# Retention of seven batch entries in 64x64 array tiles, with half of the heads shifted by 64 tokens

## The chip, the cores and the metric

The kernel runs on one core of a Trainium2 chip. A core has five engines with instruction queues of their own: TensorE (matmuls into PSUM), VectorE, ScalarE and GpSimd (element-wise work), and SyncE (here only DMA issue). They meet through semaphores. The metric is the device time of one execution in microseconds (us); lower is better. The kernel before takes 315.73 us (median of 3 runs, 315.45 to 316.26).

## The reference

Two layers follow one another. The first is a retention, an attention without a softmax, over 8 batch entries, 8 heads, 576 tokens and a head width of 64:

```
scores = q @ k^T / sqrt(64)
D[i, j] = gamma_h ** (i - j)  if i >= j  else 0,   gamma_h = 1 - 2 ** (-5 - h)
x       = (scores * D) @ v            # per batch entry and head
```

The heads of a token are then laid side by side, which gives x as 4608 tokens by 512. The second layer is an MLP:

```
h = x @ w_in          # 512 -> 2048
g = h * sigmoid(1.702 * h)
out = g @ w_out       # 2048 -> 512
```

All inputs and the output are float32; the kernel computes its matmuls in bf16.

## The kernel before, in words

**Retention.** A batch entry b is worked in five chunks c of 128 tokens (the last has 64), which makes 40 steps n = 5b + c. The decay gamma^(i-j) is split: v is scaled by gamma^(-j)/8 (`scale_v`, L249 to L255), and the result for token i is scaled by gamma^i when it leaves PSUM (`evac_o`, L348 to L355). Within a chunk, `scores` (L273) multiplies keys by queries, `mask_s` (L286) zeroes what lies above the diagonal, and `values` (L294) multiplies by the scaled v. What earlier chunks contribute comes through a 64x64 state per head, k^T v, which `values` accumulates in PSUM over the chunks of an entry ("state", L316); ScalarE copies it to SBUF (`evac_z`, L344), and the next chunk multiplies it by its queries ("inter", L327). Each state pair of two heads lies block-diagonally in a 128x128 tile `zs`, so that inter is four full matmuls. k and q must be transposed first: in steps 0 to 13 by TensorE (`transposes`, L257, then `evac_t` by ScalarE, L270), from step 14 on by DMAs that SyncE issues (`dma_turn`, L357).

**Tile shapes on TensorE.** Scores use 64 rows by 128 columns of the array, two matmuls side by side (L282); masked scores times v and state use 128 rows by 64 columns, again in pairs (L303, L316); inter, transposes and the MLP use the full array.

**MLP.** It runs over nine blocks of 512 tokens. `hidden` (L400) computes 128 of the 2048 hidden features for a block, four matmuls, and ScalarE applies the activation. `project` (L438) makes a quarter of the sum for 128 output rows, four matmuls; after the fourth quarter VectorE copies the result to SBUF and SyncE stores it.

**Order.** Every engine's queue is written out by hand, by the order of the calls; the helper `Rec` derives the waits from what each operation reads and writes, and drops a wait between two operations of TensorE. `burst(n)` (L383) puts a retention step between MLP units: scores and mask of step n, values of step n-1, the transposes of a later step, the evacuation of step n-1, and `scale_v(n+1)`. Steps 0 to 3 run first; then hidden of block 0, with no burst; then the projection of block 0, with steps 4 to 7 between its 16 units (the table `between`, L541); then hidden of block 1 in halves, with bursts 8 to 13 (L548); then `region(c)` for blocks 2 to 8, which interleaves the projection of block c-1 with hidden of block c and spreads the bursts that the next block needs evenly over 32 units. The projection of block 8 ends the kernel.

**Loads.** GpSimd issues all loads (`load`, L177, one DMA of 128 tokens and 8 heads for each of q, k, v; `load_w_in`, L187, four DMAs; `load_w_out`). Slots for three batch entries exist (`NST`); entry b+3 is loaded when entry b is finished. Between w_in(1) and w_in(2) GpSimd itself scales v of steps 1 to 3.

## Time and profile before

| | |
|---|---|
| median of 3 runs | 315.73 us (315.45 to 316.26) |
| profiled execution | 314.2 us, its span 312.3 us, granted clock 0.999 |
| TensorE busy | 304.2 us, 97% of the span |
| VectorE, ScalarE, GpSimd busy | 119.6, 131.7, 110.5 us |
| hidden (L407, L425) on the chain that ended last | 34.2% + 1.4% and 3.1% + 1.4% of the span |
| projection (L441) on it | 34.3% + 4.1% + 1% |
| retention matmuls on it (L282, L303, L316, L327, L264) | 3.5%, 3.7%, 1%, 2.8%, 1.6% |
| DMA engines | busy over 90% in the first 22 of 40 slices, 20 to 30% or less after |

A row of a timeline gives the start in us from the span's start, the length in us, the engine, the line of the kernel, the operation, the tiles (out<-in), the shape and the count of instructions that are merged in it; for a matmul 64*128 are the rows and columns of the array that it uses, and the last shape is what streams through. Square brackets hold idle time before the row and what ended it. In the list of waits the three numbers are the total in us, how often, and the longest. Matmuls overlap: a single one of 512 columns lasts 379 ns from start to end, but the next starts 216 ns after it, so the times of a stage are read from starts.

### The profile page before, as it was taken

How to read it: one execution, taken by the hardware profiler on the slowest of the kernel's cores; microseconds unless marked ns; L12 is line 12 of the kernel's file. 1: busy time of each engine (PE TensorE's matmuls, PEld its weight loads, DVE VectorE, ACT ScalarE, POOL GpSimd, SP SyncE). 2: the span in 40 equal slices, each digit the busy share in tenths (PEclk: the TensorE clock that was granted, in tenths of full speed). 3: DMA queues.
4: the chain of work that ended last, by engine and by line, in shares of the span. 5: the costliest groups of instructions: out<-in, count | busy, mean ns of one | idle time of the engine just before them, and what ended most of it. 6: DMA issues, size and time to landing. Idle time of an engine off the chain costs nothing.

```text
span 312.3 us, 5547 instructions
## 1 busy us (share of the span) xinstructions
PE 304.2 (97%) x2379; PEld 154.9 (50%) x2379; DVE 119.6 (38%) x177; ACT 131.7 (42%) x241; POOL 110.5 (35%) x138
## 2 busy tenths in 40 slices
PE   7889999999999999999999999999999999999995
PEld 3444456887544444444444444444444444444442
DVE  5650068655354333333354333333353331110011
ACT  8676235776434443444433333434444443333300
POOL 9999798788566765333400000000000000000000
PEclk9999999999999999999999999999999999999999
DMA  9999999999999999999992223213230010001011
GB/s 72 150 201 202 183 151 203 174 151 149 130 167 173 173 162 175 166 161 129 174 118 42 74 64 83 60 53 83 69 92 36 34 37 34 34 36 66 35 69 67
DMA packets 148697, 34.59 MB, mean 111 GB/s; under 512 B 139968, under 2 KB 144064, under 8 KB 148672
## 3 DMA queue, kind: packets, MB, share of 16 engines
q0 software_dynamic: 116736, 18.36, 88.2%
q1 hardware_dynamic: 31936, 15.87, 23.4%
q8 instruction: 19, 0.31, 0.4%
q14 instruction: 6, 0.05, 0.0%
HBM read 36.70 MB, written 9.44 MB: 148 GB/s over the span
## 4 chain that ended last, share of the span: by engine, by line
PE 92%; POOL 3%; DMA 2%; issue 0%; ACT 0%; DVE 0%; POOLq 0%
PE psU L441 34%; PE psH L407 34%; PE psH L441 4%; PE psO L303 4%; PE psS L282 4%; PE psH L425 3%; PE psO L327 3%; DMA w_in_sb<-in_moe_w_in_dram 2%; PE psT L264 2%; PE psU L425 1%; PE psU L407 1%; POOL st_q L184 1%; POOL st_k L184 1%; PE psZ L316 1%; PE psO L441 1%; POOL st_v L184 1%
## 5 line engine op out<-in xcount | busy, mean ns | idle before, releaser
L412 ACT ACTIVATE gT<-psH 128x512 bf16<-128x512 f32 x123 | 73.6, 598 | 129.2 <-PE psH L407 129.2
L407 PE MATMUL psH<-xT,w_in_sb 128*128 128x512 bf16 x492 | 120.9, 379 | 1.1 <-DMA w_in_sb<-in_moe_w_in_dram 1.1
L441 PE MATMUL psU<-w_out_sb,gT 128*128 128x512 bf16 x496 | 121.9, 379 | 0.0
L291 DVE TENSOR_TENSOR sm<-psS,mask 128x1024 bf16<-128x1024 f32 (+1 forms) x40 | 44.7, 1116 | 100.1 <-PE psS L282 100.1
L407 PEld LDWEIGHTS psH<-xT,w_in_sb 128*128 128x128 bf16 x492 | 47.5, 98 | 57.0 <-DVE xT L353 1.1
L441 PEld LDWEIGHTS psU<-w_out_sb,gT 128*128 128x128 bf16 x496 | 47.4, 98 | 53.6 <-ACT gT L412 0.3
L184 POOL DMA_DIRECT2D st_k<-in_k_dram x40 | 34.8, 870 | 27.0 <-PE psO L327 17.6
L449 DVE COPY osb<-psU 128x512 f32<-128x512 f32 x31 | 21.4, 691 | 55.6 <-PE psU L441 54.7
L184 POOL DMA_DIRECT2D st_q<-in_q_dram x40 | 35.0, 875 | 10.6 <-issue 10.2
L184 POOL DMA_DIRECT2D st_v<-in_v_dram x40 | 34.8, 874 | 8.1 <-issue 4.7
L254 DVE TENSOR_TENSOR st_v<-st_v,vfac 128x512 bf16<-128x512 bf16 x37 | 25.2, 681 | 18.3 <-DMA st_v<-in_v_dram 18.3
L344 ACT ACTIVATE zs<-psZ 64x256 bf16<-64x256 f32 x64 | 24.2, 378 | 12.4 <-PE psZ L316 11.4
L353 DVE TENSOR_TENSOR xT<-psO,gq 128x512 bf16<-128x512 f32 (+1 forms) x38 | 23.8, 627 | 5.6 <-PE psO L327 4.9
L270 ACT ACTIVATE qk<-psT 128x1024 bf16<-128x1024 bf16 x14 | 14.4, 1025 | 17.5 <-PE psT L264 17.5
L282 PEld LDWEIGHTS psS<-qk 64*128 64x128 bf16 x320 | 8.7, 94 | 17.2 <-issue 12.3
L282 PE MATMUL psS<-qk 64*128 64x128 bf16 (+1 forms) x320 | 15.0, 213 | 1.6 <-ACT qk L270 1.6
L303 PE MATMUL psO<-sm,st_v 128*64 128x128 bf16 (+1 forms) x304 | 14.9, 220 | 0.0
L441 PE MATMUL psH<-w_out_sb,gT 128*128 128x512 bf16 x64 | 14.8, 379 | 0.0
L425 PE MATMUL psH<-xT,w_in_sb 128*128 128x256 bf16 x88 | 11.4, 273 | 0.0
L303 PEld LDWEIGHTS psO<-sm,st_v 128*64 128x64 bf16 x304 | 9.2, 109 | 4.3 <-issue 0.6
L327 PE MATMUL psO<-qk,zs 128*128 128x128 bf16 (+1 forms) x120 | 11.0, 215 | 0.0
L441 PEld LDWEIGHTS psH<-w_out_sb,gT 128*128 128x128 bf16 x64 | 6.1, 98 | 7.2 <-ACT gT L412 0.3
(57 smaller groups left out, 127.6 us busy)
## 6 DMA issues: line engine op xcount, KB each, us to landing
out_dram<-osb SPq DMA_DIRECT2D x36, 256.0 KB, 2.2
st_q<-in_q_dram POOLq DMA_DIRECT2D x32, 128.0 KB, 17.3
st_k<-in_k_dram POOLq DMA_DIRECT2D x32, 128.0 KB, 17.3
st_v<-in_v_dram POOLq DMA_DIRECT2D x32, 128.0 KB, 17.3
w_in_sb<-in_moe_w_in_dram POOLq DMA_DIRECT2D x4, 512.0 KB, 8.4
w_out_sb<-in_moe_w_out_dram POOLq DMA_DIRECT2D x4, 512.0 KB, 13.8
st_q<-in_q_dram POOLq DMA_DIRECT2D x8, 64.0 KB, 18.7
st_k<-in_k_dram POOLq DMA_DIRECT2D x8, 64.0 KB, 18.6
```

What stands on the lines that cost most here:

```text
L184: R.op("POOL", lambda e, d=d, s=s: e.dma_start(d, s), w=[(nm, sl, c)], dma=(nm, sl, c))
L254: R.op(eng, lambda e: e.tensor_tensor(t, t, f, ALU.mult), r=["vfac"], w=[("v", sl, c)])
L282: i = e.matmul(psS[:, hh, hp, 0:N], t[rows, 1, hp, :], t[rows, 0, hp, 0:N])
L291: R.op("DVE", lambda e: e.tensor_tensor(o, i, m, ALU.mult), r=["mask"], w=[("sm", n % 3)], ps=["S"])
L303: i = e.matmul(po[64 * hh : 64 * hh + 64, hp, 0:N], st_v[:, sl, c, 64 * h : 64 * h + 64], sm[n % 3][:, hh, hp, 0:N], start=(hp == 0), stop ...
L344: R.op("ACT", lambda e, rows=rows: e.activation(zs[c % 2][rows, :, rows], psZ[rows, :, 0:64], AF.Copy), w=[("zs", c % 2, hh)], ps=["Z"])
L353: R.op("DVE", lambda e: e.tensor_tensor(xT[:, :, t0 : t0 + N], po[:, :, 0:N], gq[:, c, :, 0:N], ALU.mult), r=[("gq", min(c, 1))], w=[("xT" ...
L407: i = e.matmul(bank.ap(), w_in_sb[:, a, 128 * f : 128 * f + 128], xT[:, a, 512 * c : 512 * c + 512], start=(a == 0), stop=(a == 3))
L412: R.op("ACT", lambda e: e.activation(gT[c % 2][:, f, :], bank.ap(), AF.Gelu_apprx_sigmoid), w=[("gT", c % 2, f)], ps=[key])
L425: m = e.matmul(bank[:, 256 * i : 256 * i + 256], w_in_sb[:, a, 128 * (f + i) : 128 * (f + i) + 128], xT[:, a, a0 : a0 + 256], start=(a == ...
L441: i = e.matmul(bank, gT[c % 2][:, f, 128 * r : 128 * r + 128], w_out_sb[:, f, :], start=(f == 0), stop=(f == NF - 1))
L449: R.op("DVE", lambda e: e.tensor_copy(osb[m].ap(), bank), w=[("osb", m)], ps=[key])
```

## The change

Batch entry 0 keeps its form, but for the order of heads and for inter, which becomes eight matmuls of 128x64 instead of four full ones. For entries 1 to 7:

- k and v of heads 4 to 7 are loaded 64 tokens late, each load in two DMAs of four heads: rows 64 to 127 of a chunk's slot hold the first 64 tokens of the chunk for these heads, rows 0 to 63 of the next slot its second 64. So the first half of the keys of heads 0 to 3 lies in the upper 64 partitions while that of heads 4 to 7 lies in the lower ones, and matmuls of both groups use different quarters of the array at the same time.
- `scores` works in 64x64 tiles: first 64 keys by 128 queries, then the second 64 keys by the last 64 queries; the quarter of the square above the diagonal is left out. It needs the transposed k of step n+1 too. `mask_s` uses two masks.
- `values_quarters` puts masked scores times v, state and inter of a step in two parts (first and second 64 keys), all in 64x64 tiles. The scores of the next step stand between them, and the second part waits for the first by a semaphore of TensorE itself (`own`). It needs v and k of chunk c+1 too.
- The state of one chunk alone is made in PSUM; VectorE adds it up over the chunks in `zacc` (float32) and copies it to `zq` (bf16). ScalarE no longer takes part.
- The order: 15 steps are transposed by TensorE instead of 14; transposes and DMA transposes are asked with one step more to go; steps 4 to 9 stand at other units. `burst(n)` holds `values_quarters(n-1)`, with `scores(n)` in its middle.
- w_in is loaded in four DMAs for each former one (its rows are reordered with the heads), and w_in(1) moves behind GpSimd's scaling of v. Each `load` of k or v of entries 1 to 7 is two DMAs, not one.
- VectorE makes a second mask, a second set of scale factors, and zeroes of two tiles at the start.

The core of the diff:

```diff
-PE_TURNS = 14
+PE_TURNS = 15
+        if own:
+            deps.append(own)
-            elif d.eng == eng and eng in ("PE", "SP"):
+            elif d.eng == eng and eng in ("PE", "SP") and d is not own:
...
+        def load_shifted(b, c, nm, src, dst):
+            sl = b % NST
+            parts = []
+            for u, (lo, hi) in enumerate(((0, ROWS[c]), (64 if c == 0 else 0, 128))):
+                d = dst[lo:hi, sl, c, 256 * u : 256 * u + 256].rearrange("p (h d) -> p h d", d=DH)
+                t0 = 128 * c - 64 * u
+                s = src[b, 4 * u : 4 * u + 4, t0 + lo : t0 + hi, :].rearrange("h p d -> p h d")
+                parts.append((d, s))
+            R.op("POOL", lambda e: [e.dma_start(d, s) for d, s in parts],
+                 w=[(nm, sl, c)], dma=(nm, sl, c), parts=2)
...
         def load_w_in(i):
-            s = moe_w_in.rearrange("(a p) n -> p a n", p=128)[:, :, 512 * i : 512 * i + 512]
-            R.op("POOL", lambda e: e.dma_start(w_in_sb[:, :, 512 * i : 512 * i + 512], s),
-                 w=[("w_in", i)], dma=("w_in", i))
+            parts = []
+            for u in range(2):
+                for t in range(2):
+                    d = w_in_sb[64 * t : 64 * t + 64, 2 * u : 2 * u + 2, 512 * i : 512 * i + 512]
+                    r0 = (4 * u + 2 * t) * DH
+                    s = moe_w_in[r0 : r0 + 2 * DH, 512 * i : 512 * i + 512]
+                    parts.append((d, s.rearrange("(j p) n -> p j n", j=2)))
+            R.op("POOL", lambda e: [e.dma_start(d, s) for d, s in parts],
+                 w=[("w_in", i)], dma=("w_in", i), parts=4)
...
+            def quarters_fn(e):
+                for last in range(1 if c == 4 else 2):
+                    for t in range(2):
+                        for u in range(2):
+                            keys = later if u and last else now
+                            kb = half(u ^ last)
+                            for j in range(2):
+                                i = e.matmul(psS[kb, j, 2 * t + u, 64 * last : N],
+                                             keys[half(j), 1, 2 * u + t, kb],
+                                             now[half(j), 0, 2 * u + t, 64 * last : N])
+                return i
...
+            def part(last):
+                def fn(e):
+                    if c < 4 or last == 0:
+                        for j in range(2):
+                            for u in range(2):
+                                rows, cc = half(u ^ last), c + (u & last)
+                                for t in range(2):
+                                    h = 4 * u + 2 * t + j
+                                    i = e.matmul(psV[half(t), u, 128 * j + 64 * last : 128 * j + N],
+                                                 st_v[rows, sl, cc, 64 * h : 64 * h + 64],
+                                                 s[rows, j, 2 * t + u, 64 * last : N],
+                                                 start=(last == 0 and j == 0), stop=False,
+                                                 skip_group_check=True)
+                    if c < 4:
+                        ...
+                                    i = e.matmul(psV[half(j), u, 256 + 64 * t : 320 + 64 * t],
+                                                 st_k[rows, sl, cc, hs], st_v[rows, sl, cc, hs],
+                                                 start=False, stop=False, skip_group_check=True)
+                    if c > 0:
+                        for u in range(2):
+                            j = u ^ last
+                            for t in range(2):
+                                i = e.matmul(psV[half(t), u, 128 * j : 128 * j + N],
+                                             zq[(c - 1) % 2][half(j), 2 * u + t, :],
+                                             qk[n % NQK][half(j), 0, 2 * u + t, 0:N],
+                                             start=False, stop=(last == 1), skip_group_check=True)
+                    return i
+                return fn
+            ...
+            first = R.op("PE", part(0), r=r, ps=["O", "Z"])
+            if n + 1 < NSTEP:
+                intra(n + 1)
+            R.op("PE", part(1), r=r, ps=["O", "Z"], own=first)
...
+            if n >= NC:
+                ...
+                if c == 0:
+                    R.op("DVE", lambda e: e.tensor_copy(acc, new), w=["zacc"], ps=["O", "Z"])
+                elif c < 3:
+                    R.op("DVE", lambda e: e.tensor_tensor(acc, acc, new, ALU.add),
+                         w=["zacc"], ps=["O", "Z"])
+                if c < 3:
+                    R.op("DVE", lambda e: e.tensor_copy(z, acc), r=["zacc"], w=[("zq", c % 2)])
+                else:
+                    R.op("DVE", lambda e: e.tensor_tensor(z, acc, new, ALU.add),
+                         r=["zacc"], w=[("zq", c % 2)], ps=["O", "Z"])
+                return
...
         def burst(n):
-            if n < NSTEP:
+            if n > NC:
+                values_quarters(n - 1)
+            else:
                 intra(n)
-            values(n - 1)
-            if n + 1 < PE_TURNS:
-                transposes(n + 1)
-                evac_t(n + 1)
+                values(n - 1)
+            if n + 2 < PE_TURNS:
+                turn(n + 2)
...
         load_w_in(0)
-        load_w_in(1)
         for n in range(1, 4):
             scale_v(n, "POOL")
-        load_w_in(2)
-        load_w_in(3)
+        for i in range(1, 4):
+            load_w_in(i)
...
-        between = {6: lambda: turn(4), 8: burst_4, 10: lambda: burst(5), 11: lambda: burst(6),
-                   13: burst_7}
+        between = {5: turn_4, 6: burst_4, 8: lambda: turn(6), 10: lambda: burst(5),
+                   11: lambda: burst(6), 13: burst_7}
```

In the new order `turn_4` is turn and scaling of step 4, `burst_4` the scores of step 4 with turn and scaling of step 5, and `burst_7` the values of step 6 with the scores of step 7, the evacuation, the turn of step 9 and the scaling of step 8.

## The prediction

> **What bounds the kernel now.** I read the page first, then TensorE's waits, then its timeline at one retention step of the steady part, then VectorE's timeline where steps are packed, then the loads.
>
> Page: engines, and the chain that ended last.
> ```profile
> span 312.3 us, 5547 instructions
> PE 304.2 (97%) x2379; PEld 154.9 (50%) x2379; DVE 119.6 (38%) x177; ACT 131.7 (42%) x241; POOL 110.5 (35%) x138
> ...
> PE 92%; POOL 3%; DMA 2%; issue 0%; ACT 0%; DVE 0%; POOLq 0%
> ```
> What TensorE waited for in the whole span:
> ```profile
> PE psS L282 <- ACT qk L270: 1.6, 4, 0.6
> PE psH L476 <- DVE idle L206: 1.2, 1, 1.2
> PE psH L407 <- DMA w_in_sb<-in_moe_w_in_dram: 1.1, 1, 1.1
> ```
> TensorE is the bound: it waits under 5 us, all before 47 us. Time saved in its queue is time saved, unless a wait takes its place. One steady step, TensorE's timeline (start, length, line, tiles, count):
> ```profile
> 206.50 0.59 PE L407 MATMUL psH<-xT,w_in_sb 128*128 128x512 bf16 x2
> 207.02 0.40 PE L282 MATMUL psS<-qk 64*128 64x128 bf16 x8
> 207.35 0.41 PE L303 MATMUL psO<-sm,st_v 128*64 128x128 bf16 x8
> 207.60 0.29 PE L316 MATMUL psZ<-st_v,st_k 128*64 128x64 bf16 x8
> 207.82 0.40 PE L327 MATMUL psO<-qk,zs 128*128 128x128 bf16 x4
> 208.06 0.38 PE L441 MATMUL psU<-w_out_sb,gT 128*128 128x512 bf16 x1
> ```
> The second L407 starts at 206.50+0.59-0.38 = 206.71; such a matmul occupies 0.216 us (eight in 1.73 us), so the array is free at 206.93, and the next MLP matmul starts at 208.06: the step costs 1.13 us. Subtracting a matmul's own 0.216, 0.219 and 0.196 us gives the last starts of each group. Four pairs of 128 columns (L303) go by at 0.06 us a pair, pairs of 64 columns (L316) at 0.031 (three intervals in 0.094). Between groups of unlike tile shape lies 0.09 us (206.93 to 207.02; L282 to L303; L316 to L327): three switches, 0.28 us of the 1.13. Read alike, the five steps of a batch cost now: 0.80 (burst n with n%5=0), 0.89 (1), 1.13 (2), 1.13 (3), 1.02 (4).
>
> VectorE between 54 and 57 us:
> ```profile
> 54.43 1.22 DVE L291 TENSOR_TENSOR sm<-psS,mask 128x1024 bf16<-128x1024 f32 x1 [0.52 <-PE psS L282]
> 55.57 0.68 DVE L353 TENSOR_TENSOR xT<-psO,gq 128x512 bf16<-128x512 f32 x1
> 56.17 0.68 DVE L254 TENSOR_TENSOR st_v<-st_v,vfac 128x512 bf16<-128x512 bf16 x1
> ```
> 2.4 us a step. There a step comes every 3.3 to 4.2 us, in the steady part every 6 to 8. GpSimd's timeline, and the list of DMA issues from 23 to 35 us (count, size, median us to landing):
> ```profile
> 11.96 1.60 POOL L189 DMA_DIRECT2D w_in_sb<-in_moe_w_in_dram  x2
> 13.98 3.08 POOL L254 TENSOR_TENSOR st_v<-st_v,vfac 128x512 bf16<-128x512 bf16 x3 [0.42 <-DMA st_v<-in_v_dram]
> ```
> ```profile
> st_k<-in_k_dram POOLq DMA_DIRECT2D x4, 128.0 KB, 16.4
> ```
> Loads land 16 us after issue though issued 0.87 apart: the DMA engines set the landing, not GpSimd. k of entry 1 lands at 40.7, 43.4, 46.0, 48.9 and 51.6 (issue plus 16.4 to 17).
>
> **The change, steady part (bursts 14 to 40).** Price of a group of four 64x64 tiles: no row has the shape. From below, all four run together, as both pairs of rows (L282) and pairs of columns (L303) do: 0.06 us per 128 columns, 0.031 per 64. From above, two at a time: 0.12 and 0.062. I take the lower: the two pairings use different sides of the array, and a pair's starts lie 4 ns apart, so four need 14 of the 31 ns. Then a burst with values of chunk 1 or 2:
> - switch in 0.09;
> - first part 0.24: two 128-column groups of masked scores times v, two 64-column state groups, one 128-column group of inter;
> - scores 0.18: two groups of 128 and two of 64 columns, where the masked half is gone;
> - wait of the second part on the first: its last matmul ends 0.16 after its slot, a waiting engine starts 0.04 to 0.06 later (8.17 to 8.23 after L270), the scores cover 0.18: 0.05 with the refill. Behind it stand the second part and all MLP work;
> - second part 0.18 (four 64-column groups, one of 128); switch out 0.09.
>
> Sum 0.84 against 1.13: -0.28, twice per batch. Chunk 0 (no inter): 0.72 against 0.89, -0.17. Chunk 3 with the 64-row scores, which cover less of the wait (0.15 bare): 0.84 against 1.02, -0.18. Chunk 4: 0.54 against 0.80, -0.25. Per batch -1.16; bursts 15 to 39 -5.8; burst 14 -0.2, burst 40 (nothing in its wait) +0.1: **-5.9**.
>
> A rule of the Trainium skill speaks against this: "TensorE: Matmul & The Clock Gate", section "Wait — 56ns, not 53.3ns?", lets no two matmuls start less than about 25 ns apart. By it the 56 matmuls of such a burst would take 1.4 us, and the kernel would end near 332 us. L316 starts eight in 0.094 us, 13 ns apart, so the floor does not hold across tiles.
>
> ScalarE loses L344 (24.2 us), which nothing waits for in the steady part. VectorE gains two operations for chunks 0 to 2, one for chunk 3: 128x256, 0.42 us each by L353's 128x256 form at most, 0.27 by the memset of that size at least; I take 0.42+0.35. At a step every 6 to 8 us the idle VectorE hides it. The transposing DMAs are asked one step earlier; at 200 to 250 us they land 2.5 us after issue: hidden.
>
> **The change, before 82 us.** Batch 0's inter goes from four full matmuls to four column pairs, same time, and lies before the w_in landing. New constants on VectorE (8 small operations and 2 memsets, about 2 us) fit the 2.8 us that it idles before 8.7.
>
> w_in: each of four loads becomes four, and three now stand behind GpSimd's scaling (13.98 to 17.06). An issue takes 0.87 for 1024 rows and 0.68 for 512; by that slope 0.5 for 128, by no slope 0.8. With 0.5, GpSimd is at w_in(1) at 17.4 and done with it at 19.5, landing near 22.3; it is needed at 23.0. First MLP matmul +0.2 (0 to 0.8). The twelve extra DMAs and the split k and v loads each cost the engines 0 to 0.15 us: I shift the loads by 0.8 (0.2 to 2).
>
> Bursts 6 to 13 save by the same table -1.9; the turn of step 14 joins TensorE, 0.45: **-1.5**.
>
> New waits, 38 to 77 us. scale_v(n+1), last of VectorE's step, was used two bursts later; now the next burst's first part needs it, since chunk n+1's lower half enters. So mask, evacuation, two state operations and scaling (2.4+0.75 = 3.2 us from the scores) must fit between neighbouring scores and first part. Between bursts 5 and 6 lies one unit (0.86) and a turn; also two output copies: 0.8 wait. Bursts 6 to 7, two units: 0.7. Bursts 8 to 9, two half units of 0.87: 0.65. Elsewhere three: 0 to 0.1. Turns are also asked earlier: turn(4) 0.86 earlier meets its landing, 0.5; scores(4) one unit, not two, after their turn, while ScalarE needs 1.03: 0.35; turn(6), reached at 43.6, against 43.4+0.8: 0.6; turn(8) 0.2. Together **+3.9** (1.5 to 6.5).
>
> Burst 14 needs step 15's k, whose DMA is issued after burst 12 (72.7) instead of a burst later than needed; a turn's two DMAs are issued 1.25 us apart, and those issued between 66 and 100 us land 7.2 to 9.2 after issue (median 7.6): k at 81.2 to 83.2, needed at 81.2: **+1.0** (0 to 2).
>
> Sum: 0.2-1.5+3.9+1.0-5.9 = **-2.3**. The profiled execution took 314.2 (span 312.3); the median of the runs is 315.7, 1.5 above it. 314.2-2.3 is 311.9, as a median **313.4**.
>
> **Rivals.**
> - Two at a time: a burst of chunk 1 or 2 has six 128-column and eight 64-column groups, +0.6 less the wait that this hides, so about +0.27 against before; per batch +1.1 instead of -1.16, +11 over the steady part, +2.5 early: **327**. For: no 64x64 tile in the trace. Against: both kinds of pair overlap.
> - Weights: 64-column groups as slow as 128-column ones, because a 64-column weight load takes 110 ns (L303) and four are wanted per 31 ns. +0.03 for some seven groups a burst: +5.5 steady, +0.9 early: **319.8**. It decides against the change from 10 ns a group on (2.3 us over some 240 groups). Against: L316's loads already overlap in pairs.
> - Loads: an issue costs 0.8 whatever its size. w_in ends 3 us later in the queue, hidden(0) starts 0.6 late and waits 0.6 for w_in(1), k of chunks 3 and 4 lands 1.7 late, 2.7 more in all: **316.1**, no change.
> - The waits before 82 us turn out hidden (state operations at 0.27, no DMA shift): 1.5 instead of 4.9: **310.0**.
>
> **How the numbers follow.** Forecast 0.52 (own range 311 to 316), two at a time 0.10, weights 0.14, loads 0.14, waits hidden 0.10. Under 0.3% (1 us) a measurement can't tell from no change. Faster: 0.40 of the forecast, 0.10, 0.01 of the weights: 0.51. Same: 0.07 and 0.06: 0.13. Slower: 0.36. Range 310 to 320, which leaves out the first rival and some of the second.
>
> **What would show it.** Per steady burst the MLP gap 0.84 instead of 1.13; 64*64 matmuls starting 4 ns apart in fours; a second part starting 0.21 us after the first's last slot; TensorE waits on scale_v in bursts 6, 7 and 9, on st_k before 50 us and on qk near 82. Wrong if a 64-column group takes over 0.04, or if waits on VectorE persist in the steady part.

## The result, and the profile after

The kernel after takes 319.62 us (median of 4 runs, 318.45 to 320.56) against 315.59 us for the kernel before beside it on the same chip: a ratio of 1.0132, with a 95% interval of 1.0083 to 1.0182. The forecast was faster, 313.4 us; it came out slower. The profiled execution took 318.45 us with a span of 316.6, so the span grew by 4.3 us where the prediction's sum said -2.3.

The kernel's lines have moved: scores are L331 (old form) and L342 (64x64), values L381, L393 and L400, the mask L362, scale_v L301, the transposes L311, hidden L554, project L588, the output copy L596, the state's sum and its bf16 copy L472 to L479, w_in's load L220.

From the page of the kernel after: span, engines, and the chain that ended last.

```profile
span 316.6 us, 7233 instructions
PE 301.2 (95%) x3187; PEld 150.4 (47%) x3187; DVE 137.4 (43%) x235; ACT 112.2 (35%) x186; POOL 159.7 (50%) x220
...
PE 81%; POOL 9%; DMA 5%; DVE 3%; issue 0%; POOLq 0%
```

TensorE is busy 3.0 us less than before, and yet the span is longer: the chain now goes 9% through GpSimd (3% before), 5% through a DMA and 3% through VectorE. What TensorE waited for, in the kernel after (total us, times, longest):

```profile
PE psT L311 <- DMA st_k<-in_k_dram: 2.7, 2, 2.5
PE psV L381 <- DVE st_v L301: 2.3, 3, 0.9
PE psH L554 <- DMA w_in_sb<-in_moe_w_in_dram: 1.9, 2, 1.5
PE psS L331 <- ACT qk L317: 1.6, 4, 0.6
PE psU L554 <- DMA w_in_sb<-in_moe_w_in_dram: 1.5, 1, 1.5
```

Before, the list had 1.6 us on ScalarE, 1.2 at the start and 1.1 on w_in. New are waits on k, above all of entry 0's last chunk (2.7), and on scale_v (2.3); w_in costs 2.3 us more. All of this lies before 67 us; behind it nothing is listed at all.

One retention step of the steady part in the kernel after, the same step (n%5 = 2) as the prediction read at 206.5 us; TensorE's timeline, with start, length, line, tiles and count:

```profile
211.01 1.03 PE L554 MATMUL psH<-xT,w_in_sb 128*128 128x512 bf16 x4
211.96 0.31 PE L381 MATMUL psV<-sm,st_v 64*64 64x128 bf16 x8
212.10 0.23 PE L393 MATMUL psV<-st_v,st_k 64*64 64x64 bf16 x8
212.16 0.23 PE L400 MATMUL psV<-qk,zq 64*64 64x128 bf16 x4
212.22 0.34 PE L342 MATMUL psS<-qk 64*64 64x128 bf16 x16
212.46 0.26 PE L381 MATMUL psV<-sm,st_v 64*64 64x64 bf16 x8
212.55 0.23 PE L393 MATMUL psV<-st_v,st_k 64*64 64x64 bf16 x8
212.61 0.23 PE L400 MATMUL psV<-qk,zq 64*64 64x128 bf16 x4
212.77 0.60 PE L588 MATMUL psU<-w_out_sb,gT 128*128 128x512 bf16 x2
```

The last L554 starts at 211.01+1.03-0.38 = 211.66 and frees the array 0.216 later, at 211.87. The next MLP matmul starts at 212.77: the step costs 0.90 us, where it cost 1.13. Two groups of four 128-column tiles (L381 at 211.96 to L393 at 212.10) and two of four 64-column tiles (L393 to L400) take 0.14 and 0.06 us. Four tiles do run together.

So the steady part is faster, and the time was lost earlier. Where it went, read from the starts of the same work in the two traces (burst 14 is the first burst of the steady part; the MLP matmul ahead of it ends at 78.78 us before and 86.04 after):

| stretch | change of the span |
|---|---|
| to the start of the projection of block 0 (33.39 us before, 36.22 after) | +2.8 |
| turn(4) and turn(5) waiting for k | +2.7 |
| three waits on scale_v, 53 to 66 us | +2.3 |
| all else from there to burst 14 | -0.5 |
| burst 14 to the end (233.5 us before, 230.6 after) | -3.0 |
| sum | +4.3 |

The first two rows are the loads. Busy time by stretches of 4 us in the kernel before and in the kernel after; the last three columns are TensorE's granted clock, the DMA engines' busy share and the GB/s that they moved:

```profile
16.00:20.00 4.00, 2.62 (x45) 1.62 (x43) 3.37 (x6) 3.51 (x8) 4.00 (x6) 1.00 1.23 204
20.00:24.00 4.00, 4.00 (x20) 1.84 (x19) 0.67 (x2) 2.51 (x5) 4.00 (x7) 1.00 1.23 199
24.00:28.00 4.00, 4.00 (x21) 1.77 (x19) 0.00 (x0) 2.85 (x5) 4.00 (x6) 1.00 1.23 202
28.00:32.00 4.00, 4.00 (x20) 1.86 (x19) 0.00 (x0) 2.67 (x6) 4.00 (x5) 1.00 1.24 205
```

```profile
16.00:20.00 4.00, 2.14 (x65) 1.56 (x58) 3.27 (x5) 3.36 (x7) 4.00 (x7) 1.00 0.68 100
20.00:24.00 4.00, 3.63 (x16) 1.49 (x16) 0.97 (x2) 2.32 (x6) 4.00 (x8) 1.00 1.08 149
24.00:28.00 4.00, 3.63 (x16) 1.49 (x16) 0.00 (x0) 2.41 (x5) 4.00 (x7) 1.00 1.07 111
28.00:32.00 4.00, 2.70 (x13) 1.29 (x14) 0.00 (x0) 1.64 (x3) 4.00 (x7) 1.00 1.18 188
```

Before, the engines moved some 203 GB/s without a break. After, they fall short by 104, 50, 91 and 17 GB/s in these four stretches. Times 4 us that is 1,050 KB, or 5.2 us of a queue that moves 203 GB/s. Everything behind it in the queue comes later by that much: k of entry 0's chunk 4 lands at 43.93 us instead of 38.46 (the last completion of that load in the trace), which is 5.5 us, and turn(4) waits for it.

GpSimd's timeline in the kernel after shows what feeds that queue:

```profile
11.96 2.49 POOL L220 DMA_DIRECT2D w_in_sb<-in_moe_w_in_dram  x4
14.33 3.22 POOL L301 TENSOR_TENSOR st_v<-st_v,vfac 128x512 bf16<-128x512 bf16 x3
17.36 7.25 POOL L220 DMA_DIRECT2D w_in_sb<-in_moe_w_in_dram  x12
24.41 3.23 POOL L225 DMA_DIRECT2D w_out_sb<-in_moe_w_out_dram  x4
```

While GpSimd scales v (3.2 us), one quarter of w_in is queued instead of two, about 2.6 us of transfer; then twelve issues come 0.6 us apart. The landings of the four quarters were 19.4, 22.0, 24.5 and 27.1 us before and are 20.2, 24.1, 29.3 and 32.5 after.

### The profile page after: what moved, and what is told of

Same layout as the page of the kernel before. It is cut to its first block, busy times and chain, and to the rows that moved or that the text cites. A ratio compares the mean times of both kernels' runs of the same rounds, so it can differ in the third digit from the quotient of the medians.

```text
span 316.6 us, 7233 instructions
## 1 busy us (share of the span) xinstructions
PE 301.2 (95%) x3187; PEld 150.4 (47%) x3187; DVE 137.4 (43%) x235; ACT 112.2 (35%) x186; POOL 159.7 (50%) x220
## 4 chain that ended last, share of the span: by engine, by line
PE 81%; POOL 9%; DMA 5%; DVE 3%; issue 0%; POOLq 0%
PE psU L588 33%; PE psH L554 31%; DMA st_k<-in_k_dram 5%; PE psV L381 4%; PE psH L588 3%; POOL w_in_sb L220 3%; PE psH L572 3%; PE psS L342 2%; POOL st_q L196 1%; POOL st_k L196 1%; POOL st_v L196 1%; PE psT L311 1%; PE psV L400 1%; DVE sm L362 1%; PE psU L572 1%; PE psV L588 1%
## 5 line engine op out<-in xcount | busy, mean ns | idle before, releaser
L554 PE MATMUL psH<-xT,w_in_sb 128*128 128x512 bf16 x492 | 121.2, 379 | 1.9 <-DMA w_in_sb<-in_moe_w_in_dram 1.9
L588 PE MATMUL psU<-w_out_sb,gT 128*128 128x512 bf16 x496 | 122.2, 380 | 0.0
L362 DVE TENSOR_TENSOR sm<-psS,mask 128x1024 bf16<-128x1024 f32 (+1 forms) x40 | 44.7, 1117 | 88.3 <-PE psS L342 85.3
L209 POOL DMA_DIRECT2D st_k<-in_k_dram x70 | 78.9, 1535 | 4.6 <-PE psV L400 4.3
L209 POOL DMA_DIRECT2D st_v<-in_v_dram x70 | 79.0, 1544 | 0.0
L554 PEld LDWEIGHTS psH<-xT,w_in_sb 128*128 128x128 bf16 x492 | 47.2, 98 | 58.4 <-DMA w_in_sb<-in_moe_w_in_dram 2.5
L588 PEld LDWEIGHTS psU<-w_out_sb,gT 128*128 128x128 bf16 x496 | 46.2, 98 | 56.0 <-DVE osb L596 3.7
L196 POOL DMA_DIRECT2D st_q<-in_q_dram x40 | 64.1, 1601 | 0.0
L596 DVE COPY osb<-psU 128x512 f32<-128x512 f32 x31 | 21.3, 687 | 48.8 <-PE psU L588 48.8
L301 DVE TENSOR_TENSOR st_v<-st_v,vfac 128x512 bf16<-128x512 bf16 x37 | 25.2, 681 | 23.7 <-DMA st_v<-in_v_dram 23.7
L317 ACT ACTIVATE qk<-psT 128x1024 bf16<-128x1024 bf16 x15 | 15.4, 1024 | 23.9 <-PE psT L311 23.9
L494 DVE TENSOR_TENSOR xT<-psV,gq 128x512 bf16<-128x512 f32 (+1 forms) x35 | 21.9, 627 | 4.2 <-PE psV L400 4.2
L381 PE MATMUL psV<-sm,st_v 64*64 64x64 bf16 (+1 forms) x504 | 17.5, 214 | 2.4 <-DVE st_v L301 2.3
L381 PEld LDWEIGHTS psV<-sm,st_v 64*64 64x64 bf16 x504 | 9.1, 104 | 17.2 <-issue 11.9
L588 PE MATMUL psH<-w_out_sb,gT 128*128 128x512 bf16 x64 | 14.8, 379 | 0.0
L393 PE MATMUL psV<-st_v,st_k 64*64 64x64 bf16 x448 | 13.0, 192 | 0.0
L400 PE MATMUL psV<-qk,zq 64*64 64x128 bf16 (+1 forms) x224 | 12.6, 215 | 0.1
L342 PE MATMUL psS<-qk 64*64 64x64 bf16 (+1 forms) x504 | 11.3, 203 | 0.0
L220 POOL DMA_DIRECT2D w_in_sb<-in_moe_w_in_dram x16 | 9.7, 728 | 0.0
```

Source lines behind the costliest of these rows:

```text
L196: R.op("POOL", lambda e, d=d, s=s: e.dma_start(d, s), w=[(nm, sl, c)], dma=(nm, sl, c))
L209: R.op("POOL", lambda e: [e.dma_start(d, s) for d, s in parts], w=[(nm, sl, c)], dma=(nm, sl, c), parts=2)
L220: R.op("POOL", lambda e: [e.dma_start(d, s) for d, s in parts], w=[("w_in", i)], dma=("w_in", i), parts=4)
L301: R.op(eng, lambda e: e.tensor_tensor(t, t, f, ALU.mult), r=[("vfac", min(b, 1))], w=[("v", sl, c)])
L362: R.op("DVE", lambda e: e.tensor_tensor(o, i, m, ALU.mult), r=[("mask", 0), ("mask", 1)] if b else [("mask", 0)], w=[("sm", n % 3)], ps=["S"])
L381: i = e.matmul(psV[half(t), u, 128 * j + 64 * last : 128 * j + N], st_v[rows, sl, cc, 64 * h : 64 * h + 64], s[rows, j, 2 * t + u, 64 * la ...
```

## Experiments on the loads of w_in

Two parts of the change touch w_in: its quarters are cut into four DMAs each (**size**), and w_in(1) stands behind GpSimd's scaling (**place**). Four kernels test them: size undone, place undone, both undone, and both put into the kernel before.

**Size undone.**

```diff
 def load_w_in(i):      # one DMA again, order of the kernel after
-    parts = [four pieces of 64 partitions by 2 by 512]
+    s = moe_w_in.rearrange("(a p) n -> p a n", p=128)[:, :, 512 * i : 512 * i + 512]
```

> The changed kernel, but each quarter of w_in comes in one DMA of 128 partitions as before the change (its rows then are not in the new order of heads, so the output is not the reference's; the work is the same); it keeps its place behind GpSimd's scaling. Theory W (the sixteen small DMAs of w_in, and their later place, hold up everything that is loaded after them): w_in(1) lands near 22.5 us, no MLP matmul waits at 24 and 29 us, w_out and entry 0's last chunk land some 3 to 5 us sooner than in the changed kernel, and the time falls by 4 to 5.5 us, to 314 to 315.6. Rival K (the split loads of k and v, and that they are needed a step earlier, cost the time before 82 us): only the waits on w_in themselves go (0.6+0.35+1.5 us), the wait of 2.5 us on st_k stays: about 317.

Measured: 316.67 us, ratio to before 1.0047 (1.0018 to 1.0075), span 314.7. No wait on w_in is left in TensorE's list; the quarters land at 19.1, 22.8, 25.3 and 27.9 us, but turn(4) still waits 2.6 us for k. This is what the rival K had said (about 317, the wait on k stays), not theory W; the run with both undone, below, decides between them.

**Place undone.**

```diff
 load_w_in(0)
+load_w_in(1)
 for n in range(1, 4):
     scale_v(n, "POOL")
-for i in range(1, 4):
-    load_w_in(i)
+load_w_in(2)
+load_w_in(3)
```

> The changed kernel, w_in still in sixteen DMAs, but w_in(1) issued ahead of GpSimd's scaling of v, as before the change. If the place is what counts (the DMA engines run dry between 18 and 20 us): w_in(1) lands at 22 to 22.5, the later loads 2 to 5 us sooner, time 314.5 to 317. If the size of the pieces is what counts: the packets stay slow between 21 and 28 us, scaling now ends later and delays values(3), time 318 to 320. Rival K: at most 1 us, 318.6 or more.

Measured: 318.02 us, ratio 1.0090 (1.0058 to 1.0122). The time lies where the expectation put size (318 to 320), but the edit does more than one thing: eight issues of 0.6 us now stand ahead of the scaling, so a matmul of the values waits for GpSimd's scaling. In the list of TensorE's waits of this run, and in its busy time by 2 us (last again the granted clock, the DMA share and GB/s):

```profile
PE psU L426 <- POOL st_v L301: 2.4, 1, 2.4
```

```profile
22.00:24.00 2.00, 1.73 (x5) 0.64 (x6) 1.58 (x4) 0.96 (x4) 2.00 (x5) 0.50 1.06 157
24.00:26.00 2.00, 2.00 (x7) 0.72 (x6) 0.00 (x0) 0.81 (x2) 2.00 (x4) 0.62 1.05 78
```

TensorE was idle for 2.4 us, and its clock went to 0.50 until about 25 us, which hides what the order alone is worth. The hole in the loads has only moved, to 24 to 28 us.

**Both undone.**

> The changed kernel with both undone: w_in in one DMA per quarter (rows not in the new order of heads, output not the reference's) and w_in(1) ahead of the scaling. Theory W: first MLP matmul at 19.6, no wait on w_in later, wait on st_k of entry 0 under 0.7 us; time 313.5 to 315. Rival K: 317.

Measured: 314.13 us, ratio 0.9970 (0.9942 to 0.9999), span 312.2. The quarters land at 19.2, 21.4, 23.9 and 26.5 us, and TensorE waits 0.7 us for k instead of 2.7: theory W's figures, not the rival's 317. The MLP matmul ahead of burst 14 ends at 81.39 us. So w_in accounts for 86.04 - 81.39 = 4.65 of the 7.26 us that were lost up to there; the other 2.6 are the waits on scale_v (2.5 in this run) and small change.

**Both, and nothing else, in the kernel before.**

```diff
 # before.py, rows of w_in in their own order
 def load_w_in(i):
-    s = moe_w_in...[:, :, 512 * i : 512 * i + 512]
+    parts = [(w_in_sb[64*t : 64*t+64, 2*u : 2*u+2, cols], s[64*t : 64*t+64, 2*u : 2*u+2, cols])
+             for u in range(2) for t in range(2)]
...
 load_w_in(0)
-load_w_in(1)
 for n in range(1, 4):
     scale_v(n, "POOL")
-load_w_in(2)
-load_w_in(3)
+for i in range(1, 4):
+    load_w_in(i)
```

> The kernel before, with nothing changed but w_in: sixteen DMAs instead of four, and w_in(1) to (3) behind GpSimd's scaling, as in the changed kernel. Theory W: waits on w_in of 2 to 2.5 us, then a wait of 2 to 3 us on entry 0's last chunk: 319.5 to 321 instead of 315.6. Rival K: the waits on w_in alone, 318 or less, and no wait on st_k of more than 0.5 us.

Measured: 317.61 us, ratio 1.0078 (1.0047 to 1.0109), span +3.2. The loading of w_in alone makes the kernel before slower, without one 64x64 tile in it. It costs less here than in the kernel after and than theory W said (319.5 to 321), and the loads lose less (table below); but the longest wait on k, 1.4 us, is beyond the rival's 0.5.

**Size without 64 partitions.** Is it the pieces' number, or that each fills only half of the partitions?

```diff
 def load_w_in(i):
-    parts = [four pieces of 64 partitions by 2 by 512]
+    parts = [(w_in_sb[:, a, cols], s[:, a, :]) for a in range(4)]
```

> The changed kernel, w_in still in four DMAs a quarter and in the same place, but each of them fills all 128 partitions with one run of 512 columns (rows not in the new order of heads, output not the reference's). It tells what makes the pieces slow. If it is their number: packets of w_in go on at 130 to 150 a us, time as the changed kernel within 1 us. If it is that each fills only 64 partitions: about 200 packets a us as with one DMA a quarter, time as e1_w_in_whole, 2.5 to 3 us below the changed kernel.

Measured: 318.15 us, ratio 1.0114 (1.0078 to 1.0150), the quarters at 19.1, 25.5, 28.1 and 30.8 us. That is near the kernel after, as expected if it is the number; that each piece fills half of the partitions is not the cause. Here too TensorE idled 2.1 us (for w_in(1)) and its clock went to 0.58 and 0.56 between 26 and 30 us.

**The same small pieces, with no break ahead of them.** The scaling of steps 1 to 3 moves to VectorE; w_in keeps its sixteen DMAs and its reordered rows.

```diff
-load_w_in(0)
-for n in range(1, 4):
-    scale_v(n, "POOL")
-for i in range(1, 4):
+for i in range(4):
     load_w_in(i)
...
 evac_o(0, third[0])
+for n in range(1, 4):
+    scale_v(n)
 evac_z(0)
```

> The changed kernel, w_in in its sixteen DMAs, but VectorE scales v of steps 1 to 3, so that GpSimd issues w_in(0) to (3) without a break. Theory W: no hole in the packets between 17.5 and 20 us, w_in(1) lands at 22.5 to 23.5 instead of 24.1, everything behind it 2 us sooner; 1.5 to 2.5 us faster than the changed kernel; the first MLP matmul stays near 20. If the place costs nothing: no difference.

Measured: 315.13 us, ratio to before 1.0016 (0.9993 to 1.0039), span 313.4; the quarters land at 19.1, 21.9, 24.5 and 27.1 us. Against the kernel after (1.0132) that is some 3.6 us less, more than the 1.5 to 2.5 expected. GpSimd's issues of w_in (sixteen in one go, 0.60 us each) and the busy time by stretches in this run:

```profile
11.94 9.60 POOL L220 DMA_DIRECT2D w_in_sb<-in_moe_w_in_dram  x16
```

```profile
16.00:20.00 4.00, 2.18 (x72) 1.75 (x68) 3.93 (x6) 3.09 (x7) 4.00 (x8) 1.00 1.13 168
20.00:24.00 4.00, 3.93 (x19) 1.83 (x20) 1.46 (x3) 2.73 (x6) 4.00 (x7) 1.00 1.24 202
24.00:28.00 4.00, 4.00 (x20) 1.82 (x19) 0.00 (x0) 2.71 (x5) 4.00 (x7) 1.00 1.23 202
28.00:32.00 4.00, 4.00 (x21) 1.82 (x19) 0.00 (x0) 2.90 (x5) 4.00 (x7) 1.00 1.25 205
```

The same sixteen pieces move at 202 GB/s, as the four whole loads did before. So small pieces are not slow in themselves. In the kernel after they were slow behind a break in GpSimd's issues.

The Trainium skill, "DMA: Bandwidth & Descriptors", section "Bandwidth", advises DMAs of at least 1 MiB and gives small ones a lower rate. Whole quarters of w_in read 1 MB, the pieces a quarter of that. The run with the scaling on VectorE does not show that rule: its pieces move at 202 GB/s from 20 to 28 us, whole quarters in the kernel before at 199 and 202. Behind the break the two differ as the rule has it: 149 and 111 GB/s with pieces, 204 and 196 with whole quarters (table).

The same reading for the runs with the same order of work in this stretch, from the GB/s of these four stretches against before (missing GB/s times 4 us, divided by 203), beside the landing of k of entry 0's last chunk:

| kernel | GB/s in 16-20, 20-24, 24-28, 28-32 us | queue time lost | k lands later by |
|---|---|---|---|
| after | 100, 149, 111, 188 | 5.2 us | 5.5 us |
| four pieces of 128 partitions | 110, 126, 159, 203 | 4.2 us | 4.7 us |
| before with w_in's loading alone | 132, 119, 165, 203 | 3.8 us | 4.0 us |
| whole quarters | 102, 204, 196, 184 | 2.4 us | 2.6 us |
| scaling on VectorE | 168, 202, 202, 205 | 0.7 us | 1.0 us |

With whole quarters behind the break there is one short stretch and then the full rate at once. With pieces behind the break the rate stays low for 8 to 12 us. GpSimd offers a piece of 128 KB every 0.60 us, 218 GB/s, hardly more than the 203 that the engines move, so a backlog cannot come back quickly. That would explain why the rate doesn't rise above the supply. It doesn't explain why it falls below it. In the kernel after all twelve issues are over at 24.6 us (its timeline above), and yet only 68 GB/s move from 26 to 28 us. From 24 to 28 us the engines' busy share is 1.07 where it was 1.23 before, with half of the bytes moved. So each packet takes longer: 483 packets in 4 us of 16 engines at 1.07 are 142 ns each, against 92 ns in the run with the scaling on VectorE (853 at 1.23). An empty queue may account for the hole near 18 us (23 GB/s from 18 to 19), but not for what follows; nor can GpSimd's scaling as such, which is over at 17.6 us. What holds up the packets was not settled.

## Experiments on the steady part and on VectorE

**The place of the scores.** The prediction let the scores cover the second part's wait on the first.

```diff
 first = R.op("PE", part(0), r=r, ps=["O", "Z"])
-if n + 1 < NSTEP:
-    intra(n + 1)
 R.op("PE", part(1), r=r, ps=["O", "Z"], own=first)
+if n + 1 < NSTEP:
+    intra(n + 1)
```

> The changed kernel, but the scores of the next step stand after the second part of the values, not between the parts, so that nothing covers the second part's wait on the first. In the changed kernel a last matmul of the first part starts at 212.17 us, the second part at 212.46, 0.29 later, of which scores fill 0.18 and 0.07 is bare. Theory S (the self-wait is a drain of the array, 0.23 us a step, and the scores cover most of it): a step with full scores costs 0.17 us more (1.07 instead of 0.90), one with the 64-row scores 0.06 more; over 35 steps 5 to 5.5 us slower than the changed kernel. Rival (the array drains anyway where the shape of the work changes): no difference, 0.90 as before.

Measured: 328.14 us, ratio 1.0437 (1.0391 to 1.0483). A steady step with values of chunk 1 or 2 costs 1.08 us instead of 0.90. TensorE's timeline at such a step of this run:

```profile
219.07 0.23 PE L400 MATMUL psV<-qk,zq 64*64 64x128 bf16 x4
219.37 0.26 PE L381 MATMUL psV<-sm,st_v 64*64 64x64 bf16 x8
...
219.58 0.35 PE L342 MATMUL psS<-qk 64*64 64x128 bf16 x16
```

The last matmul of the first part starts at 219.07+0.23-0.22 = 219.08 and occupies 0.06; the second part starts at 219.37. The bare wait is 0.23 us, which is what the prediction had put together for it (0.18 covered by the scores and 0.05 left). In the kernel after the second part starts just as long after the first, 0.29 us (212.17 to 212.46), but with the scores in between. Against the kernel after the run loses more than the 5 to 5.5 us expected: its span is 9.4 us longer. The steps with values of chunks 4 and 0 lose 0.26 and some 0.24 us, more than the 0.17 expected, and another part is VectorE's: the mask comes later in its step, the waits on scale_v grow to 3.3 us, and output copies are waited for 2.0 us (eight times).

**Output copies on ScalarE.** In the kernel after the MLP stream itself has seven gaps of 0.12 us and one of 0.18 that were not there before, 1.0 us in all, each some 4.4 us after the start of a retention step. The page names them at the weight loads of project (busy, mean ns, then the idle time before and what ended most of it), and VectorE's timeline shows the step that is behind one of them, at 114.4 us:

```profile
L588 PEld LDWEIGHTS psU<-w_out_sb,gT 128*128 128x128 bf16 x496 | 46.2, 98 | 56.0 <-DVE osb L596 3.7
```

```profile
110.75 1.23 DVE L362 TENSOR_TENSOR sm<-psS,mask 128x1024 bf16<-128x1024 f32 x1 [2.35 <-PE psS L342]
111.89 0.68 DVE L494 TENSOR_TENSOR xT<-psV,gq 128x512 bf16<-128x512 f32 x1
112.49 0.41 DVE L474 TENSOR_TENSOR zacc<-zacc,psV 128x256 f32<-128x256 f32 x1
112.94 0.29 DVE L477 CAST zq<-zacc 128x256 bf16<-128x256 f32 x1
113.15 0.68 DVE L301 TENSOR_TENSOR st_v<-st_v,vfac 128x512 bf16<-128x512 bf16 x1
113.75 0.68 DVE L596 COPY osb<-psU 128x512 f32<-128x512 f32 x1
```

The copy that frees psU stands behind a whole step of VectorE. The two new operations (L474, L477: 0.66 us from 112.49 to 113.15) push it beyond the moment when TensorE wants the bank again.

```diff
-R.op("DVE", lambda e: e.tensor_copy(osb[m].ap(), bank), w=[("osb", m)], ps=[key])
+R.op("ACT", lambda e: e.activation(osb[m].ap(), bank, AF.Copy), w=[("osb", m)], ps=[key])
```

> The changed kernel, but ScalarE, which has lost the state copies, copies the MLP's output blocks out of PSUM instead of VectorE. Theory V (VectorE's longer step makes psU free late: some ten gaps of 0.12 us in the MLP's stream four units after a step, and part of the waits on scale_v before 70 us): gaps gone, 1.2 us, and 0.5 to 1 us of the early waits; 1.5 to 2.5 us faster than the changed kernel. Rival (the gaps are TensorE's own, instruction fetch): they stay, no difference within 0.7 us, or slower where ScalarE now holds up the hidden banks.

Measured: 317.48 us, ratio to before 1.0081 (1.0042 to 1.0120). All gaps are gone, and burst 14 to the end takes 229.4 us instead of 230.6. (By the ratios it is 0.5% faster than the kernel after, but their intervals overlap; the 1.2 us are read from the traces.)

**Scaling on VectorE, output copies and the state's bf16 copy on ScalarE.**

```diff
 # the two edits above, and
 if c < 3:
-    R.op("DVE", lambda e: e.tensor_copy(z, acc), r=["zacc"], w=[("zq", c % 2)])
+    R.op("ACT", lambda e: e.activation(z, acc, AF.Copy), r=["zacc"], w=[("zq", c % 2)])
```

> The kernel after with the two edits that helped so far put together (scaling of steps 1 to 3 on VectorE, output copies on ScalarE), and the conversion of the summed state to bf16 of chunks 0 to 2 moved to ScalarE too. Theory V (VectorE's step is too long: it makes TensorE wait 0.12 us behind eight output copies, and 0.6 to 0.8 us behind scale_v in three early bursts): the 0.12 us gaps go (about -1.2 us against the run with the scaling moved alone, which stood at 1.0016 of before), the three waits on scale_v shrink by about 0.3 us each; about 312.5 to 313.5, ratio to before 0.992 to 0.997. Rival (ScalarE, which also runs the activation after every hidden unit, becomes the late one): the gaps return as waits on ScalarE and the time is 315 or more, ratio 1.00 or above.

Measured: 314.77 us, ratio to before 0.9995 (0.9973 to 1.0018), above the forecast range. The waits on scale_v fell from 2.2 us in the run with the scaling alone to 1.1, but 1.1 us of waits on ScalarE took their place behind 82 us: theory and rival were both half right. Burst 14 to the end took 230.2 us.

**scale_v ahead of the mask.**

```diff
 def burst(n):
+    if 8 <= n < NSTEP - 1:
+        scale_v(n + 1)
     if n > NC:
         values_quarters(n - 1)
 ...
     finish(n - 1)
-    if n + 1 < NSTEP:
+    if n < 8:
         scale_v(n + 1)
```

> As the run with scaling on VectorE and copies on ScalarE, but from burst 8 on scale_v(n+1) stands ahead of the step's mask on VectorE instead of last in the step. Theory V: VectorE idles 0.6 to 1.7 us ahead of each mask in these bursts, so the scaling costs nothing there, and the wait of the next burst's first part on scale_v goes for bursts 8 and later (two of three, 1.0 to 1.3 us in the run with the scaling moved, less what the other edit already took): 0.3 to 1.2 us faster than without this edit. Rival (the first part then waits on the state's bf16 copy or on the evacuation instead, which stand at nearly the same place): under 0.3 us gained, and the waits come back under another line.

Measured: 314.15 us, ratio 0.9974 (0.9952 to 0.9996); 0.6 us faster in the median than without this edit, with intervals that overlap. The third wait on scale_v (0.3 us in the run before this one) is gone; in its place stands one of 0.2 us on the state's copy. TensorE's waits behind 56 us, without the lines on "issue", are in this run:

```profile
PE psH L556 <- ACT gT L561: 0.5, 2, 0.3
PE psH L556 <- ACT osb L598: 0.3, 2, 0.2
PE psU L590 <- ACT gT L561: 0.3, 2, 0.2
PE psV L381 <- ACT zq L477: 0.2, 1, 0.2
```

(This trace and the one of the run before lack 39 matmul records, mostly one behind a step, so their gaps behind steps read 0.22 us too long.) ScalarE's timeline shows why, here ahead of one of the two waits on gT, which ends at 102.68 us:

```profile
101.72 0.42 ACT L477 ACTIVATE zq<-zacc 128x256 bf16<-128x256 f32 x1 [2.13 <-DVE zacc L474]
102.04 1.07 ACT L561 ACTIVATE gT<-psH 128x512 bf16<-128x512 f32 x2
```

The state's copy waits for VectorE at the head of ScalarE's queue for 2.13 us, and two activations follow behind it without a break; TensorE waits for the first of them.

**One scaling given back to GpSimd.**

```diff
 load_w_in(0)
 load_w_in(1)
+scale_v(3, "POOL")
 load_w_in(2)
 load_w_in(3)
...
-for n in range(1, 4):
+for n in range(1, 3):
     scale_v(n)
```

> As the run with scale_v ahead of the mask, but the scaling of step 3 is given back to GpSimd, behind w_in(1). Theory Q (w_in's small pieces are slow only when the DMA queue has run dry): a hole of about 1 us behind eight queued pieces does not empty the queue, w_in keeps landing at about 24.5 and 27 us, and VectorE, which is busy without a break from 14.5 to 19.9 us, frees the last xT of block 0 0.5 to 0.7 us earlier: the first MLP matmul at 19.2 to 19.6 instead of 20.1, 0.3 to 0.7 us faster. Rival (any hole lets the queue run dry): w_in(2) and w_in(3) 2 us or more later, waits on w_in reappear, 1 to 2 us slower.

Measured: 314.31 us, ratio 0.9985 (0.9955 to 1.0014): no gain. Nine of the twelve runs took 313.2 to 314.7 us and three 316.6 to 318.8. The kernel before beside them spreads nearly as far (313.8 to 317.1), so the spread alone says nothing of the loads. The profile shows one of the three (317.59): w_in(2) lands at 27.0 us and turn(4) waits 2.5 us for k, as the rival said. But its reason was not there: w_in(1) went on landing until 21.5 us, so the queue did not run dry while GpSimd scaled (16.6 to 17.6 us), and the rate is lowest after the last issue. From GpSimd's timeline, and the busy time by 2 us:

```profile
17.64 4.95 POOL L220 DMA_DIRECT2D w_in_sb<-in_moe_w_in_dram  x8
```

```profile
24.00:26.00 2.00, 2.00 (x11) 0.88 (x9) 0.00 (x0) 1.40 (x3) 2.00 (x4) 1.00 0.92 75
```

So small pieces can be slow behind a break that leaves transfers in the queue; no run shows why. The other eleven executions were not profiled, so how often it happens stays open, and with it theory Q.

**The state's copy back on VectorE, behind step 13.**

```diff
 if c < 3:
-    R.op("ACT", ...)
+    R.op("ACT" if n < 13 else "DVE", ...)      # bf16 copy of zacc
```

> As the run with scale_v ahead of the mask, but from step 13 on the bf16 copy of the summed state goes back from ScalarE to VectorE (ScalarE keeps the output copies). Theory A (ScalarE could take the 0.6 us output copies, as the run with these alone showed, but not the state's copy besides: with both, TensorE waited some 1.1 us for ScalarE after 82 us, and the span from burst 14 to the end was 230.2 us against 229.4 with the output copies alone): the waits on ScalarE behind 82 us go, burst 14 to the end takes about 229.4 us, 0.6 to 1.0 us faster than the run with scale_v ahead, ratio to before about 0.995. Rival (VectorE's step is too long again, and the gaps come back as waits for scale_v or the evacuation): no gain, ratio 0.997 or above.

Measured: 312.95 us, ratio to before 0.9946 (0.9917 to 0.9976), the fastest kernel here, and the only one whose whole interval lies more than 0.2% below before; against the kernel after it is 0.9946/1.0132 = 0.982. There are no waits of TensorE behind 82 us, every steady step costs 0.90, 0.79 or 0.61 us, and burst 14 to the end takes 311.3 - 81.9 = 229.4 us, as expected. What it still waits for up to 60 us is, besides 0.8 us on scale_v and 0.7 on k, from its list:

```profile
PE psH L560 <- DMA w_in_sb<-in_moe_w_in_dram: 1.4, 1, 1.4
...
PE psV L381 <- issue: 0.5, 1, 0.5
```

The last line was not settled: in this run and five of the others, TensorE stands still for 0.2 to 1.3 us within values between 53 and 58 us, and the trace shows nothing that it waits for.

## Why the prediction was wrong

**Four tiles at a time: right.** The 64x64 matmuls of a group start 3.5 ns apart (4 predicted), a group of four takes 0.056 us with 128 columns and 0.031 to 0.032 with 64 (0.06 and 0.031 predicted). The rivals "two at a time" and "weights" fall.

**The steady part, -5.9: measured -3.0.** A step costs 0.90, 0.79, 0.90 and 0.61 us where the prediction had 0.84, 0.72, 0.84 and 0.54: 0.06 to 0.07 more in each. The terms: first part 0.255 for 0.24, scores 0.177 for 0.18, wait 0.066 for 0.05, second part 0.213 for 0.18, switches as said. Most of it is the second part, whose first 64-column group behind the wait takes 0.052 instead of 0.031. Over 27 bursts that is some 1.7 us. The gaps behind output copies add 1.0 to 1.2. The step that failed is "At a step every 6 to 8 us the idle VectorE hides it": idle time on average says nothing about the one operation that stands behind the step in the same queue and that TensorE waits for. The run with the copies on ScalarE showed this: from burst 14 on it took 1.2 us less.

**w_in, +0.2 (0 to 0.8), and the loads shifted by 0.8 (0.2 to 2): the error that decided.** The step was "With 0.5, GpSimd is at w_in(1) at 17.4 and done with it at 19.5, landing near 22.3". GpSimd's side was nearly right (17.36, 0.60 an issue, so done at about 19.8), the landing was 24.1, and w_in(2) and w_in(3) landed 4.8 and 5.4 us later than before. The prediction had itself read that the DMA engines set the landing and not GpSimd, but it then priced the move by issue times. It did not ask how much transfer was left in the queue while GpSimd scaled v: two quarters before, one after. The break and the slow pieces behind it cost 5.2 us of queue time; with whole quarters behind it the break cost 2.4. The prediction allowed 0.8, from 0 to 0.15 us for each extra DMA, a price that none of its rows shows. On TensorE the loss became +2.8 us up to the projection of block 0 and +2.7 at turn(4) and turn(5), where the prediction had 0.2 and, with scores(4), 0.85. Undoing place and size together brings the kernel from 1.0132 to 0.9970 of before; undoing size alone brings 1.0047, and removing the break alone 1.0016. So the two shares do not simply add: of the 1.62% that both together remove, size alone removes 0.85 and the break alone 1.16. That the loading of w_in is the cause is shown, by these runs and by its transfer into the kernel before; why small pieces are slow behind a break is not.

**The rival "loads"** named the right place, at 316.1 us, but by a mechanism that was not there: an issue cost 0.60 us, not 0.8, and with the scaling on VectorE the same number of issues cost next to nothing.

**New waits, 38 to 77 us.** The waits on scale_v were predicted at 0.8, 0.7 and 0.65 us and measured at 0.76, 0.93 and 0.61, for the reason given (scale_v is last in VectorE's step, and the next burst needs it): the edits that shorten VectorE's step halved them, and the one that puts scale_v ahead of the mask turned the last of the three, by then 0.3 us, into 0.2 us on the state's copy. scores(4) waited 0.25 us (0.35 predicted). turn(4) waited 2.5 (0.5), which is the loads again. turn(6) and turn(8) waited for nothing (0.6 and 0.2).

**Bursts 6 to 13, -1.5: measured about -0.5**, with all else up to burst 14 in it. The same 0.06 us a step makes 0.5 us of the difference; the rest was not settled.

**Burst 14, +1.0 (0 to 2): nothing.** TensorE got there 7.3 us later than before, and the transposing DMAs landed some 5.6 us after issue, not 7.6. In the fastest kernel here, which gets there 3.1 us later than before, there is no such wait either; the forecast delay was never seen.

Sum in the prediction's own terms: it had -2.3. The steady part came out 2.9 worse, the loads some 4.5, the early bursts 1.0; burst 14 and the smaller turns came out some 1.8 better. With that the sum is +4.3, as measured.

## What to carry to other kernels

When work is moved ahead of or behind a stretch in which the issuing engine does something else, count how many microseconds of transfer stand in the queue when that stretch begins. In this case the queue was late by 2.4 us behind a break of 3 us when whole quarters followed, and by 5.2 when small pieces followed that were issued one by one. Transfers left in the queue are no sure protection: in one profiled execution small pieces were slow behind a break of 1 us with work still queued. And before an operation is put on an idle engine, look for the operation behind it in that queue that the bottleneck engine waits for: the 0.66 us that VectorE took on here cost TensorE 0.12 to 0.18 us at eight places, and the state's copy on ScalarE held up activations while it waited at the queue's head.

## What the runs showed that had not been expected

- Sixteen DMAs that read a quarter megabyte each move at 202 GB/s when they are issued without a break, and at 111 to 149 GB/s for 8 us behind one of 3 us, with the same issue spacing. The slow stretch goes on when all are issued (68 GB/s from 26 to 28 us, the last issue being over at 24.6), and in one execution it came with the queue never empty (75 GB/s from 24 to 26 us).
- Behind a wait of TensorE on its own semaphore, the first group of four 64-column tiles takes 0.052 us instead of 0.031.
- TensorE's granted clock fell to 0.50 behind a wait of 2.4 us that ended at 18.0 us (w_in(1) first), behind one of 2.1 us that ended at 25.5 us (four pieces of 128 partitions), and even behind one of 1.5 us that ended at 20.3 us (output copies on ScalarE, 0.50 from 21 to 24.3 us); in the kernel after, a wait of 1.5 us that ended at 20.2 us and one of 2.5 us at 44 us left it at 1.00. The Trainium skill, "TensorE: Matmul & The Clock Gate", section "What's actually happening", has the clock halve after an idle window of about 3.4 us that runs freely. The halving agrees; here it came after shorter idle times, and not after each.
